# Head of a causal-convolution MLP: the first convolutions in 64x64 TensorE tiles, and B split like A

## The chip, the cores and the metric

One core of a Trainium2 chip (trn2) runs the whole program as one launch. The metric is device time in microseconds (us); the median of three runs before the change is 2223.6 us. Engines: PE is TensorE (matmul), PEld its weight loads, DVE VectorE, ACT ScalarE, POOL GpSimd, SP the queue that issues the transfers.

## The reference

```python
# x [8, 4096, 192], weight [8, 7]; w_in [192, 2048], w_out [2048, 192]; s, b scalars
w = softmax(weight, axis=-1)               # seven taps for each of 8 heads of 24 channels
x_unf = x_pad[:, idx, :]                   # causal: six zeros ahead of each sequence
out = np.einsum('hk,bskhg->bshg', w, x_unf).reshape(B * S, D)
h = out @ w_in
r = np.maximum(h, 0.0)
g = s * (r * r) + b
return (g @ w_out).astype(np.float32)
```

A depthwise causal convolution with seven taps along the sequence, then a two-layer MLP with a squared ReLU, all in float32.

## The kernel before

Channels lie on partitions, tokens along the free axis. The 32768 tokens are taken 1024 at a time (`Tokens(n)`, 32 of them), each as two blocks j = 0, 1 of 512. The 192 channels are A (channels 0 to 127) and B (the last 64). For B both blocks share a tile, `xB`: block 0 on partitions 0 to 63, block 1 on 64 to 127.

A product in float32 is made of three products in the fast type (fp32r): an operand is split into a high part (a cast) and a low part (operand less high part). The weights come as float64 bits, in eight pairs p of 256 hidden units, and `Widen` splits each on the chip in five steps: `magnitudes` (ACT), `top` (three DVE instructions), `his` (ACT casts), `low` (two on DVE), `los` (lows, DVE); `rest` is low and los. For pair 0 this is done in two parts, columns 0 to 383 for w_in (`w0`) and the rest for w_out (`w0out`).

`first(n, j, p)` is one product with w_in: 18 matmuls of 64 rows, two at a time in the two halves of the array, in the order A straight (`sA`), B, A swapped (`wA`). The swapped tile holds the other half of the channels on each half of the partitions; SP makes it with two transfers (`swap`). The result `h` has two buffers in PSUM, and ACT's `relu` frees one. Then `square` (ACT) and a cast make the high part, `lows` (DVE) the low part, and `second(n, j, p)` multiplies with w_out, with a lag of two results (`LAG`). `second_B` does the B columns of w_out later for n >= 2, in 64x64 tiles.

For n = 0 the weights become ready while they are used: `head()` writes out the first pairs' work by hand, and `pair(p)` the later ones: two firsts, the next pair's `rest`, ReLU, square and cast of both, `magnitudes` and `top` of the pair after, two seconds. `convolve(k)` puts k steps of the next tokens' convolution between: seven DVE instructions for A, seven for B (`accA`, `accB`), then the split. DVE, ACT, PE and, in the head, SP issue strictly in the order in which the code is written (`in_order`).

In the head before, PE convolves B and block 1 of A with diagonal 128x128 float32 weights (seven matmuls of 512 columns each, ACT makes the diagonals), DVE convolves block 0 of A, and PE makes low parts with a matmul by minus identity (`minus`). B's split for these tokens and the next (`split_B_at_once`) copies the halves of the partitions with ACT and DVE, so that `tB` and `wB` of block 0 need no transfer.

Of the kernel before, what the change touches and what calls it, by code (L numbers as in the profile page):

```python
# [9 lines left out]
F32 = mybir.dt.float32  # L10
# [7 lines left out]
P = 128  # L18
# [9 lines left out]
WARM = (BLK, BLK // 2, BLK // 2)  # L28
# [3 lines left out]
GAP = 40  # L32
# [13 lines left out]
def conv_attention_then_squared_relu_mlp(  # L46
# [96 lines left out]
    class Tokens:  # L143
# [7 lines left out]
        def load(self):  # L151
            n = self.n
            t0 = n * SUP
            self.xA = xin.tile([P, PAD + SUP], F32, name="xA")
            self.xB = xin.tile([P, PAD + BLK], F32, name="xB")
            skip = PAD if t0 % seq == 0 else 0
            if skip:
                nc.gpsimd.memset(self.xA[:, 0:PAD], 0.0)
# [28 lines left out]
        def split_A(self, j, acc):  # L187

            s = self.sA[j] = xs.tile([P, 2, BLK], F32R, name="sA", bufs=3)
            self.wA[j] = xs.tile([P, 2, BLK], F32R, name="wA", bufs=3)  # L190
            nc.scalar.copy(s[:, 0, :], acc)
            yield
            nc.vector.tensor_tensor(
                s[:, 1, :], acc, s[:, 0, :].bitcast(F32), op=ALU.subtract
            )
# [3 lines left out]
        def split_B(self, acc):

            self.tB = xs.tile([P, 2, BLK], F32R, name="tB")
            self.wB = xs.tile([P, 2, BLK], F32R, name="wB")
            hiB = xs.tile([P, BLK], F32R, name="hiB", bufs=1)
            nc.vector.tensor_copy(hiB, acc)
            yield
            for j in range(2):
                r = slice(j * DB, (j + 1) * DB)
                nc.vector.tensor_copy(self.tB[0:DB, j, :], acc[r, :])
                nc.vector.tensor_tensor(
                    self.tB[DB:P, j, :], acc[r, :], hiB[r, :].bitcast(F32), op=ALU.subtract  # L210
                )
                if j == 1:
                    self.swap(self.wB, self.tB)
                    self.begun = True
                yield

        def split_B_at_once(self, acc):

            self.tB = xs.tile([P, 2, BLK], F32R, name="tB")
            self.wB = xs.tile([P, 2, BLK], F32R, name="wB")  # L220
            hiB = xs.tile([P, BLK], F32R, name="hiB", bufs=1)
            nc.scalar.copy(hiB, acc)
            for j in range(2):
                r = slice(j * DB, (j + 1) * DB)
                places = (self.tB, self.wB) if j == 0 else (self.tB,)
                for k, to in enumerate(places):
                    nc.scalar.copy(to[k * DB :][0:DB, j, :], hiB[r, :].bitcast(F32))
                for k, to in enumerate(places):
                    nc.vector.tensor_tensor(
                        to[(1 - k) * DB :][0:DB, j, :], acc[r, :], hiB[r, :].bitcast(F32),  # L230
                        op=ALU.subtract,
                    )
                if j == 1:
                    self.swap(self.wB[:, 1, :], self.tB[:, 1, :])
                self.begun = True
                yield

        def split_tensor(self, acc, hi, meanwhile=None):

            nc.scalar.copy(hi, acc)  # L240
            if meanwhile:
                meanwhile()
            nc.tensor.matmul(acc, minus, hi, start=False, stop=True, skip_group_check=True)
            return lambda to, rows: nc.scalar.copy(to, acc[rows, :])
# [22 lines left out]
        def conv_tensor(self, acc, diag, x, taps=range(K)):  # L267

            for k in taps:
                nc.tensor.matmul(  # L270
                    acc, diag[:, k, :], x[:, k : k + BLK], start=k == 0, stop=k == K - 1
                )
# [96 lines left out]
    def room_for(dtype):  # L369
# [33 lines left out]
    def head():  # L403
# [9 lines left out]
        w0, w0out, w1 = Widen(0, 0, CI), Widen(0, CI, CT), wide[1]  # L413

        def diagonal(w):
            d = room_for(F32).rearrange("p a (k f) -> p (a k) f", f=P)
            for k in range(K):
                nc.scalar.activation(d[:, k, :], ident, AF.Identity, scale=w[:, k : k + 1])
# [18 lines left out]
        wB = one.wB = xs.tile([P, 2, BLK], F32R, name="wB")
        hiB = xs.tile([P, BLK], F32R, name="hiB", bufs=1)
        lo = one.split_tensor(accB, hiB, lambda: one.conv_tensor(acc1, diagA, one.xA[:, BLK:], range(0, 2)))
        one.conv_tensor(acc1, diagA, one.xA[:, BLK:], range(2, K))  # L440
        next(split)
        fetch(2)
# [11 lines left out]
        w1.los()
        nc.scalar.copy(tB[top, 1, :], hiB[bottom].bitcast(F32))

        def second_block():
            sA = one.sA[1] = xs.tile([P, 2, BLK], F32R, name="sA", bufs=3)
            wA = one.wA[1] = xs.tile([P, 2, BLK], F32R, name="wA", bufs=3)
            lo1 = one.split_tensor(acc1, sA[:, 0, :])  # L460
            one.swap(wA[:, 0, :], sA[:, 0, :])
            lo(tB[bottom, 1, :], bottom)
            one.swap(wB[:, 1, :], tB[:, 1, :])
            lo1(sA[:, 1, :], slice(0, P))
            one.swap(wA[:, 1, :], sA[:, 1, :])
# [29 lines left out]
    wide = {p: Widen(p, 0, CT) for p in range(1, NPAIR)}  # L495
# [82 lines left out]

    def square(at, cast):
        q, g = at  # L580
        nc.scalar.activation(q, q, AF.Square)  # L581
# [376 lines left out]
```

## Time and profile before

| | |
|---|---|
| runs | 2223.6, 2223.56, 2223.77 us; median 2223.6 |
| the profiled execution | 2224.18 us, its span 2222.4 us |
| granted TensorE clock | 1.00 |
| PE busy | 2216.2 us, 100% of the span |
| DVE busy | 1740.7 us, 78% |
| ACT busy | 1317.7 us, 59% |
| POOL busy | 303.9 us, 14% |

Times in the views are from the span's start. A busy PE is matmuls with modelled ends, so that the distance between two starts says more than the busy time. Shares over the whole span say little of the first 100 us, where the weights are made.

### The profile page before, as it was taken

The page shows a single profiled execution, that of the slowest core. Times are in us where ns is not written, and L with a number is a line of the kernel's source. Part 1 is how long each engine was busy: PE and PEld are TensorE (multiplying, and loading weights), DVE is VectorE, ACT ScalarE, POOL GpSimd, SP SyncE. Part 2 cuts the span into 40 slices and gives each one's busy share as a digit, 9 for nine tenths or more (in the row PEclk, how much of TensorE's full clock was granted, in tenths as well). Part 3 has the DMA queues.
Part 4 walks back from the last instruction along what each step waited for, and adds up shares of the span by engine and source line. Part 5 has one row for each costly group of instructions (what it writes and reads, how often), then busy time and mean ns, then how long its engine had stood idle before and what let it go on. Part 6 is the DMA issues. An engine that isn't in the chain of part 4 may idle for free.

```text
span 2222.4 us, 44638 instructions
## 1 busy us (share of the span) xinstructions
PE 2216.2 (100%) x19334; PEld 1610.3 (72%) x19334; DVE 1740.7 (78%) x1988; ACT 1317.7 (59%) x1424; POOL 303.9 (14%) x199
## 2 busy tenths in 40 slices
PE   9999999999999999999999999999999999999999
PEld 6788777777777777777877777777777777777776
DVE  8898777787777878778787777887787877878754
ACT  8759555565555665555655556555566555665554
POOL 0001111011111011111111101111111111011110
PEclk9999999999999999999999999999999999999999
DMA  5113212112121121211111111112112121121110
GB/s 181 30 36 93 56 51 58 51 47 55 47 58 48 44 58 44 58 51 51 48 53 49 53 50 47 53 49 63 46 46 57 45 58 49 46 56 39 44 30 17
DMA packets 46165, 117.49 MB, mean 53 GB/s; under 512 B 7760, under 2 KB 8016, under 8 KB 45968
## 3 DMA queue, kind: packets, MB, share of 16 engines
q1 hardware_dynamic: 45824, 114.50, 18.6%
q8 instruction: 151, 2.47, 0.5%
q14 instruction: 46, 0.38, 0.1%
q10 hardware_dynamic: 144, 0.13, 0.0%
HBM read 31.64 MB, written 25.17 MB: 26 GB/s over the span
## 4 chain that ended last, share of the span: by engine, by line
PE 97%; DVE 2%; ACT 1%; DMA 0%; issue 0%; SPq 0%; DVEq 0%
PE h L550 46%; PE acc L718 29%; PE acc L737 18%; PE acc L662 2%; PE h L737 0%; DVE accA L176 0%; DVE ql L587 0%; ACT q L581 0%; PE acc L632 0%; PE acc L638 0%; PE acc L640 0%; PE acc L639 0%; ACT q L573 0%; DMA xA<-in_xA 0%; DVE q L328 0%; DVE q L342 0%
## 5 line engine op out<-in xcount | busy, mean ns | idle before, releaser
L573 ACT ACTIVATE q<-h 128x1024 f32<-128x1024 f32 x512 | 526.0, 1027 | 562.9 <-PE h L550 561.0
L587 DVE TENSOR_TENSOR ql<-q,qh 128x1024 fp32r<-128x1024 f32 x498 | 666.6, 1339 | 56.2 <-ACT qh L583 4.8
L583 DVE CAST qh<-q 128x1024 fp32r<-128x1024 f32 x482 | 344.2, 714 | 360.9 <-ACT q L581 357.5
L718 PE MATMUL acc<-qh,W 64*128 64x512 f32 x3816 | 588.4, 386 | 0.0
L581 ACT ACTIVATE q<-q 128x1024 f32<-128x1024 f32 x512 | 543.5, 1062 | 16.1
L550 PE MATMUL h<-sA,W 64*128 64x512 f32 x3072 | 436.4, 389 | 0.0
L550 PE MATMUL h<-wA,W 64*128 64x512 f32 x3072 | 432.1, 386 | 0.0
L550 PE MATMUL h<-wB,W 64*128 64x512 f32 x1536 | 430.5, 387 | 0.0
L550 PE MATMUL h<-tB,W 64*128 64x512 f32 x1536 | 430.4, 387 | 0.0
L718 PEld LDWEIGHTS acc<-qh,W 64*128 64x128 f32 x3816 | 357.9, 184 | 75.6 <-issue 0.8
L737 PE MATMUL acc<-q,WB 64*64 64x512 f32 x3776 | 412.1, 591 | 0.0
L718 PE MATMUL acc<-ql,W 64*128 64x512 f32 x1908 | 371.7, 386 | 0.0
L550 PEld LDWEIGHTS h<-sA,W 64*128 64x128 f32 x3072 | 285.6, 184 | 83.9 <-issue 24.7
L550 PEld LDWEIGHTS h<-wA,W 64*128 64x128 f32 x3072 | 288.4, 184 | 60.2
L737 PEld LDWEIGHTS acc<-q,WB 64*64 64x64 f32 x3776 | 141.5, 133 | 254.7 <-issue 254.7
L176 DVE SCALAR_TENSOR_TENSOR accA<-xA,tap,accA 128x512 f32<-128x512 f32 x378 | 313.0, 828 | 5.7
L550 PEld LDWEIGHTS h<-tB,W 64*128 64x128 f32 x1536 | 282.8, 184 | 40.7 <-issue 0.2
L550 PEld LDWEIGHTS h<-wB,W 64*128 64x128 f32 x1536 | 282.9, 184 | 20.3
L727 POOL TENSOR_TENSOR outs<-outs 128x512 f32<-128x512 f32 x59 | 94.9, 1609 | 1223.4 <-ACT outs L726 1223.4
L718 PEld LDWEIGHTS acc<-ql,W 64*128 64x128 f32 x1908 | 179.0, 184 | 37.5
L176 DVE SCALAR_TENSOR_TENSOR accB<-xB,tap,accB 128x512 f32<-128x512 f32 x186 | 167.4, 900 | 6.3
L749 POOL TENSOR_TENSOR outs<-outs 128x512 f32<-128x512 f32 x59 | 107.2, 1817 | 199.1 <-ACT outs L748 198.8
(147 smaller groups left out, 891.4 us busy)
## 6 DMA issues: line engine op xcount, KB each, us to landing
wA<-sA SPq DMA_DIRECT2D x126, 256.0 KB, 3.6
outT<-outs SPq DMA_DIRECT2D x62, 256.0 KB, 2.0
wB<-tB SPq DMA_DIRECT2D x60, 256.0 KB, 3.4
xA<-in_xA SPq DMA_DIRECT2D x24, 515.0 KB, 3.6
outT<-outs SPq DMA_DIRECT2D x65, 128.0 KB, 2.2
xB<-in_xB SPq DMA_DIRECT2D x32, 259.0 KB, 3.0
outs<-outs SPq DMA_DIRECT2D x60, 128.0 KB, 2.7
outs<-in_w SPq DMA_DIRECT2D x7, 768.0 KB, 6.1
```

Source lines behind the costliest of these rows:

```text
L176: nc.vector.scalar_tensor_tensor(acc, src, w[:, k : k + 1], acc, op0=ALU.mult, op1=ALU.add)
L550: nc.tensor.matmul(h[:, i, :], w_in(w, p, chunk[0], rows), chunk[part], start=start, stop=stop)
L573: nc.scalar.activation(q, h, AF.Relu)
L581: nc.scalar.activation(q, q, AF.Square)
L583: cast(qh, q)
L587: nc.vector.tensor_tensor(ql, q, qh.bitcast(F32), op=ALU.subtract)
L662: nc.tensor.matmul(accs[to + 2 * i][0:cols], w(f, r), q[r, f % 2, :], start=start and f == 0, stop=stop and f == NF - 1,)
L718: nc.tensor.matmul(accs[i], w(f, r), q[r, f % 2, :], start=f == 0 and lo == 0, stop=f == ends[i] and lo == 2,)
L727: nc.gpsimd.tensor_tensor(o, o, o2, op=ALU.add)
L737: nc.tensor.matmul(accs[r.start // HB][i * DB : (i + 1) * DB], WB[r, p, i, :], q[r, i, :], start=p == 0, stop=p == NPAIR - 1, skip_group_c ...
L749: nc.gpsimd.tensor_tensor(o, o, o2, op=ALU.add)
```

## The change

The first convolutions, of A and B, all go to PE in 64x64 tiles. A diagonal needs only its two 64x64 blocks, so `diagonal` is now one DVE multiplication of 448 elements a partition. Straight tiles (rows to the same half of the output) serve A, crossed tiles (rows to the other half) serve B, one tap of both being four matmuls in the four quarters of the array. Block 1 of A is cut into two halves of 256 tokens; the second is fetched with swapped halves (`xS`), so that it too goes through crossed tiles. The weights of pair 0 are fetched ahead of the tokens, those of pair 1 ahead of A's second block, those of pair 2 before the head. The warm-up matmuls are 512 and six times 256 columns instead of 512 and two.

B is split in place like A for all tokens (`sB`, swapped by SP to `wB`): one ACT cast, one DVE subtraction, two transfers of 64 x 1024 words. Pair 2's weights are widened in two parts, in another order. `minus`, `hiB`, `tB` go; `GAP` keeps the size of the pool ahead of the others.

```diff
-WARM = (BLK, BLK // 2, BLK // 2)
+WARM = (BLK,) + 6 * (BLK // 2,)
+HALF = BLK // 2
-GAP = 40
+GAP = 160
 # Tokens.load, n == 0
+            if n == 0:
+                fetch(0, 0, CI)
             nc.sync.dma_start(self.xB, xB[n])
...
             if n == 0:
-                fetch(0, 0, CI)
-                nc.sync.dma_start(self.xA[:, cut:], xA[:, BLK:SUP])
+                fetch(1)
+                self.xS = room_for(F32).rearrange("p a b -> p (a b)")[:, 0 : PAD + HALF]
+                nc.sync.dma_start(self.xA[:, cut : cut + HALF], xA[:, BLK : BLK + HALF])
+                for i in range(2):
+                    to, of = (slice(k * HB, (k + 1) * HB) for k in (i, 1 - i))
+                    nc.sync.dma_start(self.xS[to], xA[of, BLK + HALF - PAD : SUP])
+        def lo(self, s, acc, cols=slice(0, BLK)):
+            nc.vector.tensor_tensor(
+                s[:, 1, cols], acc, s[:, 0, cols].bitcast(F32), op=ALU.subtract)
+        def split(self, kind, j, acc):
+            s, w = self.parts(kind, j)
             nc.scalar.copy(s[:, 0, :], acc)
             yield
+            self.lo(s, acc)
+            self.swap(w, s)
             yield
 # steps(): B of every later token
-                    yield from (self.split_B_at_once if self.n == 1 else self.split_B)(acc)
+                    yield from self.split("B", 0, acc)
+                    self.begun = True
+        def tap_tensor(self, acc, diag, x, k, swapped):
+            n = acc.shape[1]
+            for i in range(2):
+                r, o = (slice(h * HB, (h + 1) * HB) for h in (i, 1 - i if swapped else i))
                 nc.tensor.matmul(
+                    acc[o], diag[r, k, :], x[r, k : k + n],
+                    start=k == 0, stop=k == K - 1, skip_group_check=True,
                 )
 # head()
-        one.conv_tensor(accB, diagB, one.xB)
-        for _ in one.conv(acc0, one.xA, tapA, BLK):
-            pass
+        for k in range(K):
+            one.tap_tensor(acc0, diagA, one.xA, k, False)
+            one.tap_tensor(accB, diagB, one.xB, k, True)
+        for k in range(K):
+            one.tap_tensor(acc1[0], diagA, one.xA[:, BLK:], k, False)
+            one.tap_tensor(acc1[1], diagS, one.xS, k, True)
...
+        nc.scalar.copy(wB[:, 0, :], accB)
+        nc.scalar.copy(sA[:, 0, :], acc0)
+        one.lo(wB, accB)
+        one.lo(sA, acc0)
+        nc.sync.dma_start(sB[0:HB].bitcast(F32), wB[HB:P].bitcast(F32))
+        one.swap(wA, sA)
+        nc.sync.dma_start(sB[HB:P].bitcast(F32), wB[0:HB].bitcast(F32))
+        w1.los()
+        w2.magnitudes()
...
-        ha = first(0, 0, 0, second_block)
+        ha = first(0, 0, 0)
+        w0out.low()
+        q = relu(ha)
+        square_of(q)
         w0out.his()
-        q = relu(ha)
-        w0out.rest()
-        wide[2].magnitudes()
-        wide[2].top()
+        ha = first(0, 0, 1)
+        a1 = relu(ha)
         fetch(3)
         start_tokens(1)
         fetch(4)
-        ha = first(0, 0, 1)
-        a1 = relu(ha)
-        put(0, 0, 0, square(q, nc.vector.tensor_copy))
+        q = cast_of(q, nc.vector.tensor_copy)
+        put(0, 0, 0, q)
+        w0out.los()
         hb = first(0, 1, 0)
-        wide[2].low()
+        w2.top()
+        w2.his()
         b0 = squares(hb, nc.scalar.copy)
         put(0, 1, 0, b0)
-        wide[2].his()
-        wide[2].los()
+        w2.rest()
+        w2out.magnitudes()
+        w2out.top()
+        w2out.his()
         hb = first(0, 1, 1)
         put(0, 0, 1, square(a1, nc.scalar.copy))
+        w2out.rest()
```

The order on ACT behind the first ReLU of the head, before. L573 is `relu`, L581 `square`, L583 the cast of a squared result, L317 `magnitudes`, L335 `his`:

```order
L573 ACTIVATE q<-h 128x1024
L317 ACTIVATE q<-outs 128x768
L573 ACTIVATE q<-h 128x1024
L581 ACTIVATE q<-q 128x1024
L573 ACTIVATE q<-h 128x1024
L581 ACTIVATE q<-q 128x1024
L583 CAST qh<-q 128x1024
L335 CAST W<-q 128x640
```

And now, from the same ReLU on (L551 `relu`, L558 `square`, L567 cast, L292 `magnitudes`, L310 `his`):

```order
L551 ACTIVATE q<-h 128x1024
L558 ACTIVATE q<-q 128x1024
L310 CAST W<-q 128x256
L310 CAST q<-q 128x2x64
L551 ACTIVATE q<-h 128x1024
L310 CAST W<-q 128x384
L551 ACTIVATE q<-h 128x1024
L558 ACTIVATE q<-q 128x1024
L567 CAST qh<-q 128x1024
L292 ACTIVATE q<-outs 128x384
L310 CAST W<-q 128x256
L310 CAST q<-q 128x2x64
```

The square of the first result moved ahead of the second ReLU, and casts of pair 2's weights (the fourth and the last two L310) now stand ahead of the third ReLU and of the fourth, where before they stood behind a cast of a result.

The same place on DVE before: L583 casts the first squared result, L587 makes low parts, L328 ends pair 2's `top`, L341 and L342 are its `low`, L348 its `los`:

```order
L325 TENSOR_SCALAR q<-q 128x768
L328 SCALAR_TENSOR_TENSOR q<-outs,q 128x768
L583 CAST qh<-q 128x1024
L587 TENSOR_TENSOR ql<-q,qh 128x1024
L341 TENSOR_SCALAR q<-q 128x768
L342 SCALAR_TENSOR_TENSOR q<-outs,q 128x768
L587 TENSOR_TENSOR ql<-q,qh 128x1024
L348 TENSOR_TENSOR W<-q,W 128x640
```

And now (L567 cast, L571 lows, L323 and L325 `los`, L296 to L303 `top`, L316 `low`):

```order
L567 CAST qh<-q 128x1024
L571 TENSOR_TENSOR ql<-q,qh 128x1024
L323 TENSOR_TENSOR W<-q,W 128x256
L323 TENSOR_TENSOR q<-q 128x2x64
L325 TENSOR_TENSOR W<-W,q 128x256
L325 TENSOR_TENSOR q<-q 128x2x64
L296 TENSOR_SCALAR q<-q 128x384
L300 TENSOR_SCALAR q<-q 128x384
L303 SCALAR_TENSOR_TENSOR q<-outs,q 128x384
L571 TENSOR_TENSOR ql<-q,qh 128x1024
L316 TENSOR_SCALAR q<-q 128x384
```

Pair 2's `top` stood ahead of the cast of the first result and now stands behind it and behind the lows of pair 0's w_out.

The third place is SP at the split of B for tokens 1, before:

```order
L184 DMA wA<-sA 64x1024
L185 DMA wA<-sA 64x1024
L160 DMA xB<-in_xB 128x518
L185 DMA wB<-tB 64x512
L184 DMA wB<-tB 64x512
L163 DMA xA<-in_xA 128x1030
```

And now:

```order
L191 DMA wA<-sA 64x1024
L192 DMA wA<-sA 64x1024
L163 DMA xB<-in_xB 128x518
L191 DMA wB<-sB 64x1024
L192 DMA wB<-sB 64x1024
L166 DMA xA<-in_xA 128x1030
```

The places are the same; the two transfers of B now carry both blocks, where before block 0 had needed none.

More of the change, by code (lines that the diff above doesn't have):

```diff
@@ L185, in swap, with parts @@
             nc.sync.dma_start(to[HB:P], of[0:HB])
-        def split_A(self, j, acc):
-            s = self.sA[j] = xs.tile([P, 2, BLK], F32R, name="sA", bufs=3)
-            self.wA[j] = xs.tile([P, 2, BLK], F32R, name="wA", bufs=3)
+        def parts(self, kind, j=0):
+            s, w = (xs.tile([P, 2, BLK], F32R, name=x + kind, bufs=3 - (kind == "B")) for x in "sw")
+            if kind == "A":
+                self.sA[j], self.wA[j] = s, w
+            else:
+                self.sB, self.wB = s, w
+            return s, w
@@ L197, in split_A @@
             yield
[L199 to L244, printed above, removed]
         def half(self, j, i):
             r = slice(i * HB, (i + 1) * HB)
-            b = (self.tB, self.wB) if i == 0 else (self.wB, self.tB)
+            b = self.sB if i == j else self.wB
@@ L260, in steps @@
                 yield from self.conv(acc, self.xA[:, j * BLK :], tapA, BLK)
-                yield from self.split_A(j, acc)
+                yield from self.split("A", j, acc)
                 if j == 0:
@@ L413, in head, with diagonal @@
         w0, w0out, w1 = Widen(0, 0, CI), Widen(0, CI, CT), wide[1]
[L415 to L418, printed above, removed]
-            return d
-        top, bottom = slice(0, DB), slice(DB, P)
-        diagB = diagonal(tapB)
+        w2, w2out = Widen(2, 0, CI), Widen(2, CI, CT)
+        def diagonal(place, k):
+            d = place.rearrange("p (k f) -> p k f", f=DB)[:, 0:K]
+            shape = [P, K, DB]
+            nc.vector.tensor_tensor(
+                d, fold.unsqueeze(1).to_broadcast(shape),
+                tap[:, k, :].unsqueeze(2).to_broadcast(shape), op=ALU.mult,
+            )
+            return d
@@ L423, in head @@
+        two = room_for(F32)
+        diagA, diagB = diagonal(two[:, 0, :], 0), diagonal(two[:, 1, :], 1)
+        diagS = diagonal(room_for(F32)[:, 0, :], 2)
         accB = ps_o.tile([P, BLK], F32, name="acc2")
-        acc1 = ps_o.tile([P, BLK], F32, name="acc1")
-        one.conv_tensor(accB, diagB, one.xB)
-        acc0 = xs.tile([P, BLK], F32, name="accA")
-        for _ in one.conv(acc0, one.xA, tapA, BLK):
-            pass
-        nc.scalar.mul(minus, ident, -1.0)
-        diagA = diagonal(tapA)
+        acc0 = ps_o.tile([P, BLK], F32, name="acc1")
@@ L431, in head @@
+        acc1 = [ps_o.tile([P, BLK], F32, name=f"acc{k}")[:, 0:HALF] for k in (2, 1)]
+        for k in range(K):
[4 more added lines that the diff above has]
+            one.tap_tensor(acc1[1], diagS, one.xS, k, True)
         w0.magnitudes()
-        split = one.split_A(0, acc0)
-        next(split)
         w0.top()
         w0.his()
-        tB = one.tB = xs.tile([P, 2, BLK], F32R, name="tB")
@@ L437, in head @@
[L437 to L442, printed above, removed]
+        w0.rest()
         w1.magnitudes()
-        w0.rest()
         w1.top()
-        nc.scalar.copy(tB[top, 0, :], hiB[top].bitcast(F32))
-        nc.scalar.copy(wB[bottom, 0, :], hiB[top].bitcast(F32))
@@ L448, in head @@
-        lo(tB[bottom, 0, :], top)
-        lo(wB[top, 0, :], top)
-        w1.his()
         w1.low()
         w0out.magnitudes()
-        w0out.top()
[L454 to L465, printed above, removed]
@@ L468, in head @@
-        ha = first(0, 0, 0, second_block)
+        w1.his()
+        sB, wB = one.parts("B")
+        sA, wA = one.parts("A", 0)
+        nc.scalar.copy(wB[:, 0, :], accB)
[7 more added lines that the diff above has]
+        w2.magnitudes()
+        s1, w1A = one.parts("A", 1)
@@ L469, in head @@
+        for k, c in enumerate((slice(0, HALF), slice(HALF, BLK))):
+            nc.scalar.copy(s1[:, 0, c], acc1[k])
+        for k, c in enumerate((slice(0, HALF), slice(HALF, BLK))):
+            one.lo(s1, acc1[k], c)
+        one.swap(w1A, s1)
+        w0out.top()
+        ha = first(0, 0, 0)
+        w0out.low()
+        q = relu(ha)
+        square_of(q)
         w0out.his()
-        q = relu(ha)
-        w0out.rest()
-        wide[2].magnitudes()
-        wide[2].top()
+        ha = first(0, 0, 1)
@@ L493, in head @@
         convolve(CONV[1])
-    wide = {p: Widen(p, 0, CT) for p in range(1, NPAIR)}
+    wide = {p: Widen(p, 0, CT) for p in range(1, NPAIR) if p != 2}
     def column_sums(k):
@@ L942 @@
         "xB": xB,
[L943 removed]
+        "taps": np.ascontiguousarray(
+            np.stack([taps[:P], np.tile(taps[P:], (2, 1)), np.roll(taps[:P], P // 2, 0)], axis=1)
+        ),
         "w": np.concatenate([w_in, *w_out], axis=2),
```

35 lines of the change are left out of this document (17 added, 18 removed).

## The prediction

> **What bounds the kernel now.** I read the page's busy times first, then the chain of work that ended last, then the first 100 us engine by engine in order of time. The page's PE line, a row of the table by stage (columns: stretch, its length, busy time of PE, PEld, DVE, ACT, POOL, clock, DMA share, GB/s) and rows of the chain:
>
> ```profile
> PE 2216.2 (100%) x19334; PEld 1610.3 (72%) x19334; DVE 1740.7 (78%) x1988; ACT 1317.7 (59%) x1424; POOL 303.9 (14%) x199
> 32.70:60.00 27.30, 27.30 (x188) 20.68 (x188) 25.73 (x38) 25.70 (x30) 0.00 (x0) 1.00 0.25 84
> 30.50 0.68 PE acc L632 x2
> 288.68 13.89 PE acc L737 x128
> 302.57 2.30 PE h L550 x18
> ...
> 313.04 2.04 PE h L550 x18
> ```
>
> From about 100 us on nothing but PE counts: the chain is unbroken matmuls, a first takes 2.04 us for nine pairs, and the 0.26 us more after each second_B (2.30) is the one seam. The new kernel has the same matmuls there, so a delay or gain of the head goes to the end one to one. But from 32.7 to 60 us DVE and ACT are 94% busy beside PE, and the chain comes to PE only at 30.5 us, from DVE's lows. In the head three engines are nearly full, and order among them decides. PE's rows that I use as marks (start, length; L550 is a first, 34.89 that of pair 2's second block, 55.19 pair 5's, 91.95 the B part of the first one of tokens 1):
>
> ```profile
> 0.99 3.54 PE L410 MATMUL acc<-q 128*128 128x512 f32 x6 [0.99 <-POOL xA L158]
> 4.49 6.25 PE L270 MATMUL acc<-xB,q 128*128 128x512 f32 x14
> 34.89 0.85 PE L550 MATMUL h<-sA,W 64*128 64x512 f32 x6
> 55.19 0.84 PE L550 MATMUL h<-sA,W 64*128 64x512 f32 x6
> 91.95 0.62 PE L550 MATMUL h<-wB,W 64*128 64x512 f32 x2
> ```
>
> Six matmuls are three pairs at 0.23 us, so 0.69 us of array and 0.16 us until the last can be read. Transfers (landing of the first tokens; data rate in slices of a quarter microsecond over 0 to 10 us; two swaps with time to landing, and their issues):
>
> ```profile
> 1.65 3.79 DMA xA<-in_xA
> GB/s 0 0 0 0 0 0 0 28 34 83 58 149 166 315 379 362 389 352 438 430 332 266 274 311 328 193 205 254 336 418 406 406 442 406 467 418 394 222 124 99
> wA<-sA SPq DMA_DIRECT2D x1, 256.0 KB, 3.4
> wA<-sA SPq DMA_DIRECT2D x1, 256.0 KB, 3.7
> 12.67 0.54 SPq L184 DMA_DIRECT2D wA<-sA  x1
> 13.26 0.59 SPq L185 DMA_DIRECT2D wA<-sA  x1
> ```
>
> The second swap lands 0.59 + 3.7 - 3.4 = 0.9 us behind the first: queued swaps take 0.9 us each. ACT (casts, ReLU L573, square L581, magnitudes L317):
>
> ```profile
> 12.07 0.51 ACT L335 CAST W<-q 128x384 fp32r<-128x384 f32 x1 [0.64 <-DVE q L328]
> 20.43 0.41 ACT L335 CAST W<-q 128x256 fp32r<-128x256 f32 x1
> 20.74 0.30 ACT L335 CAST q<-q 128x128 fp32r<-128x128 f32 x1
> 21.37 1.03 ACT L573 ACTIVATE q<-h 128x1024 f32<-128x1024 f32 x1 [0.33 <-PE h L550]
> 26.62 1.06 ACT L581 ACTIVATE q<-q 128x1024 f32<-128x1024 f32 x1
> 27.71 1.05 ACT L583 CAST qh<-q 128x1024 fp32r<-128x1024 f32 x1
> 28.67 0.72 ACT L335 CAST W<-q 128x640 fp32r<-128x640 f32 x1
> 31.55 0.91 ACT L317 ACTIVATE q<-outs 128x768 f32<-128x768 f32 x1
> 32.36 1.01 ACT L573 ACTIVATE q<-h 128x1024 f32<-128x1024 f32 x1
> 33.40 1.06 ACT L581 ACTIVATE q<-q 128x1024 f32<-128x1024 f32 x1
> 88.97 0.62 ACT L222 CAST hiB<-accB 128x512 fp32r<-128x512 f32 x1 [1.95 <-DVE accB L176]
> ```
>
> Starts are 0.09 us ahead of the end before where the next does not need it. DVE (low part of A; low and los of 384 columns from 12.56 to 14.48; top of 768 and low to 18.13; top of 384 to 19.48; los of w_out from 22.26 to 23.41; cast and lows of a result):
>
> ```profile
> 11.96 0.68 DVE L193 TENSOR_TENSOR sA<-accA,sA 128x512 fp32r<-128x512 f32 x1
> 12.56 0.35 DVE L341 TENSOR_SCALAR q<-q 128x384 int32<-128x384 int32 x1
> 14.48 0.55 DVE L321 TENSOR_SCALAR q<-q 128x768 f32<-128x768 f32 x1
> 18.13 0.36 DVE L321 TENSOR_SCALAR q<-q 128x384 f32<-128x384 f32 x1
> 19.40 0.82 DVE L348 TENSOR_TENSOR W<-q,W 128x640 fp32r<-128x640 f32 x1
> 22.26 0.42 DVE L348 TENSOR_TENSOR W<-q,W 128x256 fp32r<-128x256 f32 x1
> 23.13 0.28 DVE L350 TENSOR_TENSOR q<-q 128x128 fp32r<-128x128 f32 x1
> 25.91 0.69 DVE L583 CAST qh<-q 128x1024 fp32r<-128x1024 f32 x1
> 26.63 1.23 DVE L587 TENSOR_TENSOR ql<-q,qh 128x1024 fp32r<-128x1024 f32 x1
> 32.24 1.22 DVE L587 TENSOR_TENSOR ql<-q,qh 128x1024 fp32r<-128x1024 f32 x1
> 54.50 0.82 DVE L350 TENSOR_TENSOR W<-W,q 128x640 fp32r<-128x640 f32 x1
> ```
>
> **Part 1, up to the first ReLU (R): earlier.** xA lands at 5.44 before; 384 KB of weights now stand ahead of it on SP, 1.05 us at some 375 GB/s, so 6.5. The warm-up's 1024 columns take 3.5 us; the conv's fourteen records (two a matmul) show half that price a column (6.25 us for 7 x 512), so four more of 256 end near 6.3, and PE waits little. The three diagonals have no row; the nearest, L348 with 640 columns, is 0.82 us, so I take 0.62 each for 448; they start at 3.9 and are under the wait for xA. At twice that, pair 0's top waits behind them and R comes 1.2 later; a gain is excluded by that wait.
>
> The 64x64 float32 matmul is priced by second_B: 128 records, 64 matmuls, 13.89 us, 0.217 us each with four in the array; alone it is the conv's 0.89. I take 0.217, since four quarters are used here too. So 28 x 0.217 = 6.1, to 12.6, and the half-width 28 in 3.0, to 15.7 (at no saving from the half width 18.7, R + 0.8). Low end nothing, high end is a rival below. Off PE fall 14 large matmuls and two by minus identity, off DVE 5.2 us of convolution, off ACT 14 diagonals and ten small copies: gone, but not on this path any more.
>
> Weights of pair 1 (768 KB) land at 8.5, magnitudes 0.9, top and low on DVE 14.48 to 18.13 = 3.65, so both engines are free at 13.1. Then cast of accB 0.62 (to 13.4), its low 0.68 (14.1), A's low 0.6 (14.7). SP sends B's first half at 14.1, landing 17.5, and A's two at 14.7 and 15.3, landing 18.4 and 19.3. PE does A's straight part to 16.4, waits 1.1 for B, and 1.1 for wA, ends at 20.0: **R = 20.2**, before 21.37, 1.2 us sooner. With swaps 1 us faster it is 19.2. Queued behind these swaps are only B's other half and block 1's (wanted at 22.7 and 23.4, landing by 20.2 and 22), then pair 3's weights, wanted at 37. POOL does nothing new.
>
> **Part 2, R to pair 2: much later.** Here DVE and ACT take turns. In the new order DVE's cast of the first result waits for its square; behind that cast stand its lows, los of w0out, and top of pair 2; ACT's casts of pair 2 wait for that top, and behind them stand the other block's ReLU, square and cast, for which DVE's next lows wait, and so on once more:
> - ReLU 1.04 (32.36 to 33.40) and square 1.09 (26.62 to 27.71): R + 2.15. DVE cast 0.72, lows 1.14, los 1.06, top 1.35 (18.13 to 19.48): R + 6.4.
> - ACT cast of 384 columns 0.5, ReLU 1.04, square 1.09, cast 1.05: R + 10.1. PE's second of that block starts then, at 30.3, and its low part is there at 31.5; the four firsts and one second are over at 28.6. That wait is hidden by the next.
> - DVE lows 1.14, rest of 384 columns 1.92 (12.56 to 14.48), top of w_out 1.35: R + 14.5. ACT casts 0.5, square 1.09, cast 0.96 to the next start, magnitudes 0.81, ReLU 1.01: R + 18.9.
>
> That last ReLU frees the buffer of pair 2's second first. It can start at R + 19.0 = 39.2 and started at 34.89: **4.3 us late** in spite of the sooner R, with PE idle for some 3.1 us before it.
>
> **Part 3, to pair 5.** From the lows of a1 on DVE has no gap. They start when their cast ends, R + 14.5 + 0.5 + 1.09 + 1.05 = 37.4; before, 32.24. To these 5.2 come 1.9 for the rest of w_out of pair 2, done apart now (los 1.06 and low 0.86), so DVE is 7.0 late with a small gap of before filled. Pair 5's low weights were ready at 54.50 + 0.82 = 55.32 and wanted at 55.19 + 0.46 = 55.65: slack 0.3. PE comes **6.7 us late** to pair 5. Nothing gives it back, as PE was dense from there.
>
> **Part 4, B of tokens 1.** accB is cast at 88.97; now 6.7 later, 95.7. Cast 0.62, low 0.68, to 97.0 with hand-overs. The second transfer of the swap is issued 0.55 later and lands after 3.7: 101.2. PE asks for it at 91.95 + 6.7 = 98.65 and **waits 2.6 us**, where tB and wB had needed no transfer. Bounds: nothing, if the swap were early by that much, and 3.0. Three ACT copies and two DVE subtractions fewer are off this path. For later tokens four DVE instructions fewer and one ACT cast more lie under PE's dense rows (2.04 us each), and the swap of B goes out a step sooner: nothing.
>
> **Sum.** 6.7 + 2.6 = 9.3 us, of which part 2 is 4.3, part 3 2.4. The profiled execution took 2224.18 (span 2222.4 and 1.8 around it), 0.6 over the median; with 9.3 it is 2233.5, and as a median 2232.9; I say 2233. With R, swaps and seams at their favourable ends it is 7.5, at the others 12: 2231 to 2235.6.
>
> **Rivals.** (a) Serial tiles. Both straight tiles write one bank from different halves of the rows, while second_B gives each half of the rows a bank of its own, so its row does not show this case. If two of the four wait for each other, part 1 takes 12.2 and 6.1 instead of 6.1 and 3.0: PE starts its first at 24.8, no swap is late, R = 24.8 + 2.06 + 0.16 = 27.0, 6.8 later, and all else follows: 2239.8. For it: no row with such a pair. Against: the two write different partitions. [...]
>
> (b) The clock. The opening matmuls cost twice a column for 3.5 us. If PE's wait of 3.1 us before pair 2's second block brings that state back, another 3.5 us at half speed cost 1.75: 2234.7. Before has no such wait. [...]
>
> (c) The early start is kept, and the kernel is faster. DVE is idle from pair 0's last low, about 19.5, to R + 2.15 = 22.3; if pair 2's top (1.35) were done there, ACT's casts would not wait and the firsts, ending 1 us sooner, would carry it through: 2222.6. It decides if top ends before the second ReLU does, R + 3.7 = 23.9. Against it: top stands behind the cast in the written order, and the rows of before start in that order everywhere.
>
> (d) The turns cost less: PE late by under 7.4 us in all because part 4's swap is met or DVE has slack that I don't see: 2228.1 to 2231.
>
> **How the numbers follow.** Forecast 0.70, (a) 0.12, (b) 0.06, (c) 0.04, (d) 0.08. The range leaves out (a) and (c): 2229 to 2237.5; the likeliest case's own is 2231 to 2235.6. A change under 0.2%, 4.4 us, can't be told from none. Slower holds all but (c) and a little of (d): 0.95; same 0.02, faster 0.03.
>
> **What would show it.** Right: R near 20.2; ACT's cast of 384 columns released by DVE L303 near R + 6.5; PE idle some 3 us until near 39 for the ReLU of ACT L551; pair 5's first some 6.7 us late, waiting for DVE L325; a PE wait of 2 to 3 us for the B swap near 100; equal rows after. Wrong: conv records of 64x64 spaced over 0.12 us (a), ACT's casts of pair 2 not waiting (c), or B's swap there before PE.

## The result, and the profile after

The changed kernel takes 2236.80 us (median of six runs, 2236.45 to 2237.85), the kernel before on the same chip 2223.62: a ratio of 1.006, 95% interval [1.0047, 1.0073], 13.2 us slower. The profiled execution took 2236.45 (span 2234.4), so 12.3 more than the profiled one of before and 12.0 in the span; the sums below are made against those 12.0. Two of the later kernels, the eighth and the ninth, have a profiled execution that ran at a granted clock of 0.95 and 0.75 from end to end, so it is left out of their medians.

First the page's busy times, and a table by stage, cut where the granted clock changes and 3.42 us ahead of each stretch at half clock (columns as in the prediction; the clock, as a share of full speed, stands behind POOL):

```profile
PE 2218.7 (99%) x19424; PEld 1631.9 (73%) x19424; DVE 1667.9 (75%) x1873; ACT 1324.2 (59%) x1432; POOL 304.3 (14%) x199
4.68:38.81 34.13, 28.08 (x231) 17.40 (x229) 22.74 (x45) 16.20 (x25) 0.00 (x0) 1.00 0.66 212
38.81:42.23 3.42, 1.50 (x14) 1.24 (x16) 3.20 (x8) 3.36 (x5) 0.00 (x0) 1.00 0.03 5
42.23:45.64 3.41, 3.41 (x13) 2.08 (x10) 3.34 (x5) 2.01 (x4) 0.00 (x0) 0.50 0.62 225
100.25:103.67 3.42, 1.02 (x9) 0.55 (x8) 0.74 (x1) 0.68 (x1) 0.00 (x0) 1.00 0.50 129
103.67:107.08 3.41, 3.41 (x20) 2.66 (x18) 0.00 (x0) 1.57 (x2) 0.00 (x0) 0.50 0.02 5
```

DVE does 72.8 us less than before (1740.7 to 1667.9), and the kernel is slower: what was saved lay beside PE. After each of two stretches in which PE is busy for less than half (1.50 and 1.02 us of 3.42) comes one of 3.41 us at half clock. PE's waits in the head, and its marks (the longest waits in total, then starts of firsts, now L528; 62.63 is pair 5's, 99.43 that of tokens 1):

```profile
PE h L528 <- ACT q L551: 3.0, 1, 3.0
PE h L528 <- DMA wB<-sB: 2.4, 1, 2.4
...
40.73 0.96 PE L528 MATMUL h<-sA,W 64*128 64x512 f32 x6 [3.00 <-ACT q L551]
62.63 0.70 PE L528 MATMUL h<-sA,W 64*128 64x512 f32 x4
63.97 0.51 PE L528 MATMUL h<-sA,W 64*128 64x512 f32 x2 [0.64 <-DVE W L325]
99.43 0.97 PE L528 MATMUL h<-sA,W 64*128 64x512 f32 x6
103.03 0.50 PE L528 MATMUL h<-wB,W 64*128 64x512 f32 x1 [2.40 <-DMA wB<-sB]
```

Pair 2's second block starts 5.8 us later than before (34.89), pair 5's first 7.4 (55.19), its last two straight matmuls, behind a wait for DVE, 8.3 (63.97 against some 55.65), the first one of tokens 1 8.3 (91.15 before). Then come the 2.4 of the wait, and 1.3 for the half clock behind it: seven firsts on (129.57 against 117.70), the kernel is 11.9 late, and so it stays to the end.

The turns of ACT and DVE, as the trace shows them (ACT, then DVE; the brackets give the idle time ahead and what ended it):

```profile
21.77 1.03 ACT L551 ACTIVATE q<-h 128x1024 f32<-128x1024 f32 x1 [5.36 <-PE h L528]
28.24 0.51 ACT L310 CAST W<-q 128x384 fp32r<-128x384 f32 x1 [2.94 <-DVE q L303]
36.32 0.41 ACT L310 CAST W<-q 128x256 fp32r<-128x256 f32 x1 [4.01 <-DVE q L303]
39.67 1.01 ACT L551 ACTIVATE q<-h 128x1024 f32<-128x1024 f32 x1
...
23.92 0.69 DVE L567 CAST qh<-q 128x1024 fp32r<-128x1024 f32 x1 [3.43 <-ACT q L558]
31.88 1.23 DVE L571 TENSOR_TENSOR ql<-q,qh 128x1024 fp32r<-128x1024 f32 x1 [3.67 <-ACT qh L567]
39.00 1.23 DVE L571 TENSOR_TENSOR ql<-q,qh 128x1024 fp32r<-128x1024 f32 x1 [2.71 <-ACT qh L567]
```

Whoever works, the other one is idle: DVE for 3.43, 3.67 and 2.71 us, ACT for 2.94 and 4.01.

### The profile page after: what moved, and what is told of

Read it like the earlier page. It is cut to its first block, busy times and chain, and to the rows that moved or that the text cites. A ratio compares the mean times of both kernels' runs of the same rounds, so it can differ in the third digit from the quotient of the medians.

```text
span 2234.4 us, 44704 instructions
## 1 busy us (share of the span) xinstructions
PE 2218.7 (99%) x19424; PEld 1631.9 (73%) x19424; DVE 1667.9 (75%) x1873; ACT 1324.2 (59%) x1432; POOL 304.3 (14%) x199
## 4 chain that ended last, share of the span: by engine, by line
PE 96%; DVE 2%; ACT 1%; DMA 1%; issue 0%; SPq 0%; DVEq 0%
PE h L528 46%; PE acc L702 29%; PE acc L721 18%; PE acc L646 2%; ACT q L558 0%; DVE ql L571 0%; PE h L721 0%; ACT q L551 0%; DMA outs<-in_w 0%; ACT qh L567 0%; DMA wA<-sA 0%; DVE q L303 0%; DVE q L317 0%; DMA wB<-sB 0%; ACT q L567 0%
## 5 line engine op out<-in xcount | busy, mean ns | idle before, releaser
L551 ACT ACTIVATE q<-h 128x1024 f32<-128x1024 f32 x512 | 526.2, 1028 | 557.3 <-PE h L528 555.8
L571 DVE TENSOR_TENSOR ql<-q,qh 128x1024 fp32r<-128x1024 f32 x498 | 666.5, 1338 | 63.8 <-ACT qh L567 12.3
L567 DVE CAST qh<-q 128x1024 fp32r<-128x1024 f32 x482 | 364.9, 757 | 443.7 <-ACT q L558 442.1
L558 ACT ACTIVATE q<-q 128x1024 f32<-128x1024 f32 x512 | 543.5, 1061 | 16.0
L528 PE MATMUL h<-sA,W 64*128 64x512 f32 x3072 | 443.4, 390 | 3.6 <-ACT q L551 3.0
L528 PE MATMUL h<-wA,W 64*128 64x512 f32 x3072 | 440.1, 387 | 1.1 <-DMA wA<-sA 1.1
L528 PE MATMUL h<-wB,W 64*128 64x512 f32 x1536 | 430.9, 387 | 2.4 <-DMA wB<-sB 2.4
L528 PE MATMUL h<-sB,W 64*128 64x512 f32 x1536 | 431.1, 387 | 1.6 <-DMA sB<-wB 1.6
L702 PEld LDWEIGHTS acc<-qh,W 64*128 64x128 f32 x3816 | 362.8, 184 | 74.0 <-issue 0.8
L528 PEld LDWEIGHTS h<-sA,W 64*128 64x128 f32 x3072 | 293.6, 184 | 84.7 <-issue 24.3
L528 PEld LDWEIGHTS h<-wA,W 64*128 64x128 f32 x3072 | 296.9, 184 | 59.0 <-DMA wA<-sA 1.9
L183 DVE SCALAR_TENSOR_TENSOR accA<-xA,tap,accA 128x512 f32<-128x512 f32 x372 | 308.3, 829 | 5.5
L528 PEld LDWEIGHTS h<-sB,W 64*128 64x128 f32 x1536 | 282.9, 184 | 31.4 <-DMA sB<-wB 2.0
L528 PEld LDWEIGHTS h<-wB,W 64*128 64x128 f32 x1536 | 282.8, 184 | 31.1 <-DMA wB<-sB 2.8
```

Of the source, the lines that this page charges most:

```text
L183: nc.vector.scalar_tensor_tensor(acc, src, w[:, k : k + 1], acc, op0=ALU.mult, op1=ALU.add)
L528: nc.tensor.matmul(h[:, i, :], w_in(w, p, chunk[0], rows), chunk[part], start=start, stop=stop)
L551: nc.scalar.activation(q, h, AF.Relu)
L558: nc.scalar.activation(at[0], at[0], AF.Square)
L567: cast(qh, q)
L571: nc.vector.tensor_tensor(ql, q, qh.bitcast(F32), op=ALU.subtract)
```

## The experiments

All are edits of the changed kernel, five rounds each, beside runs of the kernel before on the same chip (its medians were 2223.59, 2223.81 and 2223.61).

**1. The first turn out.**

```diff
         w0out.low()
+        w2.top()
         q = relu(ha)
...
         hb = first(0, 1, 0)
-        w2.top()
         w2.his()
```

> The changed kernel with pair 2's top for w_in (three DVE instructions, 1.35 us) moved ahead of the first result's cast, into the 3.43 us in which DVE waits for the first square. Theory A (the loss of the head is the turns of DVE and ACT, an order): the first turn goes, pair 2's second first falls from 40.73 to about 37.9, pair 5's from 62.62 to about 59.8, and the time by 2.8 us, to 2234.0; the second turn and the wait for B's swap stay, with the half clock behind the latter. Theory B (DVE simply has more to do up to pair 5, whatever the order): pair 5's first stays within 0.7 us of 62.62 and the time within 0.7 us of 2236.8.

Measured: 2235.23 us (2233.75 to 2235.83), ratio 1.0051 [1.0038, 1.0063]; 1.6 less than the changed kernel, between the two theories. The profiled execution is the slowest of the five. Its table, and PE's and ACT's rows:

```profile
15.16:18.57 3.41, 1.80 (x24) 0.92 (x16) 3.41 (x9) 0.98 (x3) 0.00 (x0) 1.00 0.63 133
18.57:25.40 6.83, 6.39 (x29) 4.22 (x29) 3.77 (x9) 2.57 (x4) 0.00 (x0) 0.50 1.00 268
...
40.21 0.96 PE L528 MATMUL h<-sA,W 64*128 64x512 f32 x6 [2.98 <-ACT q L551]
...
22.63 1.02 ACT L551 ACTIVATE q<-h 128x1024 f32<-128x1024 f32 x1 [6.11 <-PE h L528]
26.05 1.03 ACT L551 ACTIVATE q<-h 128x1024 f32<-128x1024 f32 x1 [0.81 <-PE h L528]
28.12 1.03 ACT L551 ACTIVATE q<-h 128x1024 f32<-128x1024 f32 x1 [0.64 <-PE h L528]
```

ACT's wait for pair 2's top is gone. But here PE's own firsts ran at half clock from 18.57 to 25.40, and ACT waits 0.81 + 0.64 us for them. Pair 2's second first comes 40.21 - 22.63 = 17.6 us behind the first ReLU, against 18.96 in the changed kernel: 1.4 sooner, where 2.8 were expected and 1.45 went to the slow firsts. The two quickest runs (2233.75, 2234.01) stand at the 2234.0 of theory A, but pair 5's first starts at 62.03, within theory B's 0.7 us of 62.62. By itself this run leaves theory B open; the next one does not.

**2. Both turns out.** Besides the first edit:

```diff
         w2.his()
-        b0 = squares(hb, nc.scalar.copy)
-        put(0, 1, 0, b0)
         w2.rest()
+        b0 = relu(hb)
+        square_of(b0)
         w2out.magnitudes()
+        put(0, 1, 0, cast_of(b0, nc.scalar.copy))
         w2out.top()
-        w2out.his()
         hb = first(0, 1, 1)
         put(0, 0, 1, square(a1, nc.scalar.copy))
+        w2out.his()
         w2out.rest()
```

> As the first, and the second turn taken out too: pair 2's low and lows for w_in stand ahead of the second result's lows on DVE, the magnitudes of its w_out columns ahead of that result's cast on ACT, and the casts of those columns behind the next square. Theory A: no PE wait of over 0.5 us from the firsts to pair 5 but those for a first's own result; pair 2's second first near 35.5, pair 5's near 55.5 to 56, the time 7.2 us less than the changed kernel's, 2229.6; the granted clock is 1.00 from 5 to 90 us, since the wait of 3 us is gone, and half speed only behind the wait for B's swap. Theory B: pair 5's first above 60 and the time above 2234. If the half clock is not due to the wait ahead of it, the first stretch of it is still there between 35 and 50.

Measured: 2229.77 us (2228.36 to 2232.68, nine runs), ratio 1.0027 [1.0018, 1.0037]: 7.0 less, where A said 7.2. Nothing was taken away here; the same instructions stand in another order. Theory B is out. PE's longest wait, and the table around the first ReLU and around the wait for B's swap:

```profile
PE h L529 <- DMA wB<-sB: 2.4, 1, 2.4
...
17.79:21.21 3.42, 1.85 (x11) 1.02 (x13) 3.23 (x9) 0.00 (x0) 0.00 (x0) 1.00 1.00 237
21.21:24.62 3.41, 3.41 (x20) 2.68 (x18) 0.84 (x2) 2.40 (x4) 0.00 (x0) 0.50 0.99 258
...
92.89:96.30 3.41, 2.16 (x12) 1.20 (x10) 2.18 (x4) 2.22 (x4) 0.00 (x0) 1.00 0.85 218
96.30:99.72 3.42, 2.28 (x20) 1.96 (x22) 0.00 (x0) 0.59 (x1) 0.00 (x0) 1.00 0.06 14
```

The wait for ACT's ReLU is gone, that for B's swap is as long as it was, and yet the clock stays at 1.00 behind it: it lies from 95.05 to 97.44, across two of the stretches shown, and PE is busy for 2.16 of the 3.41 us of the first (63%) and for 2.28 of the 3.42 of the second (67%). From the first wB matmul to the fourth first of these tokens it is 105.42 - 97.44 = 7.98 us, in the changed kernel 112.27 - 103.03 = 9.24: the half clock there costs **1.26 us**.

One thing expected did not come: the clock is not 1.00 from 5 to 90 us. In place of the stretch at half clock behind pair 2's wait, which is gone, there is one from 21.21, behind the waits for the first swaps. Two firsts start 25.02 - 21.54 = 3.48 us apart there instead of 2.05; pair 2's second first comes at 36.73 and pair 5's at 57.02, each 1 us or more later than expected, and pair 5's 1.1 us later than in experiment 4's trace (55.92), which has no such stretch. These 1.1 us and the 1.26 not lost behind B's wait about cancel, so that 7.0 is still a fair price of the order.

**3. No swap for the half of B that is wanted first.**

```diff
             nc.scalar.copy(s[:, 0, :], acc)
+            if kind == "B" and self.n == 1:
+                nc.scalar.copy(w[HB:P, 0, :], s[0:HB, 0, :].bitcast(F32))
             yield
             self.lo(s, acc)
-            self.swap(w, s)
+            if kind == "B" and self.n == 1:
+                nc.vector.tensor_tensor(
+                    w[HB:P, 1, :], acc[0:HB], s[0:HB, 0, :].bitcast(F32), op=ALU.subtract
+                )
+                nc.sync.dma_start(w[0:HB].bitcast(F32), s[HB:P].bitcast(F32))
+            else:
+                self.swap(w, s)
```

> The changed kernel, but for the tokens 1024 to 2047 the swapped half of B that block 0 reads is made by one more ACT copy and one more DVE subtraction (64 rows), and only the other half by a transfer. Theory A (the wait of 2.40 us for B's swap costs itself and the half clock of 3.4 us behind it): no PE wait for wB near 103, granted clock 1.00 from 99 to 110, the time 2.4 + 1.5 less, 2232.9. Theory C (the clock goes back for another reason than the wait, the load of the stage itself): the wait goes, the half clock stays, 2234.4. If the transfer is hidden anyway in the sum (another wait takes its place), no more than 1 us less.

Measured: 2233.24 us (2232.65 to 2233.76), ratio 1.0043 [1.0031, 1.0056]: 3.6 less. The table from tokens 1 on, and PE's rows there:

```profile
99.70:110.00 10.30, 10.30 (x91) 8.19 (x92) 7.62 (x12) 8.16 (x9) 0.00 (x0) 1.00 0.13 29
...
99.70 0.97 PE L536 MATMUL h<-sA,W 64*128 64x512 f32 x6
100.51 0.39 PE L536 MATMUL h<-wB,W 64*128 64x512 f32 x1
```

No wait, no half clock. The next seven firsts and what stands between them take 26.5 us as before the change; in the changed kernel they take 30.1. Theory A holds, with 1.3 us for the half clock instead of 1.5: 2.4 and 1.3, together 3.7.

**4. Both.** The edits of 2 and 3.

> The second and the third together: both turns out and B's first swapped half by copies. Theory A: the parts add, 7.2 + 3.9 less than 2236.8, 2225.7; what stays over the kernel before (about 2 us) is the first ReLU of 21.77 against a schedule made for 20.2, and there is no stretch of half clock after 5 us. Theory B: above 2231. If the two gains overlap (the swap is waited for less when the head is sooner, or DVE's split comes later), 2227 to 2228.

Measured: 2225.35 us (eleven runs; nine of them 2224.94 to 2225.81, the other two 2228.57 and 2228.78 at a mean clock of 0.998), ratio 1.0011 [1.0002, 1.0020]. 11.4 of the 13.2 us are back, with the convolutions in tiles as they were. The first one of tokens 1 starts at 92.75, 1.6 us behind the 91.15 of before, and that is nearly all that is left. Of it 0.9 us are there at the first ReLU (22.30 against 21.37); the rest comes behind it, with a wait for DVE in pair 5 (L333). PE's waits, and that ReLU:

```profile
PE h L537 <- DMA sB<-wB: 1.4, 1, 1.4
PE h L537 <- DMA wA<-sA: 1.2, 2, 0.8
PE h L537 <- DVE W L333: 0.6, 1, 0.6
...
22.30 1.03 ACT L560 ACTIVATE q<-h 128x1024 f32<-128x1024 f32 x1 [5.28 <-PE h L537]
```

**5. Why the first ReLU is late: the fetch of pair 2?**

```diff
     fetch(0, CI, CT)
-    fetch(2)
...
         w1.los()
-        w2.magnitudes()
...
         one.swap(w1A, s1)
+        fetch(2)
...
         a1 = relu(ha)
+        w2.magnitudes()
```

> The changed kernel with the 768 KB of pair 2's weights fetched behind the swaps of block 1 (and their magnitudes behind the second ReLU), so that no such transfer lands while pair 1's weights are widened. Theory D (the 1.57 us by which the first ReLU came later than forecast are mostly that landing: ACT's L292 of 768 at 1.38 us instead of 0.91, DVE's L303 of 768 at 1.22 instead of 0.96): both are back at 0.91 and 0.96, the swaps go out 0.7 to 1 us sooner, the first ReLU is near 20.9 and the time 0.8 less, near 2236. Theory E (the lateness is pair 1's own landing at 9.09 and the transfers' 4.4 us to land, with or without that fetch): durations and first ReLU stay within 0.3 us of 21.77, the time within 0.5 us of 2236.8.

Measured: 2237.53 us (2236.06 to 2238.74), ratio 1.0061 [1.0048, 1.0074]: no gain. ACT's and DVE's rows, and ACT's row of experiment 1, where that fetch was in its old place:

```profile
9.86 1.32 ACT L292 ACTIVATE q<-outs 128x768 f32<-128x768 f32 x1 [2.13 <-DMA outs<-in_w]
22.52 1.02 ACT L551 ACTIVATE q<-h 128x1024 f32<-128x1024 f32 x1 [6.12 <-PE h L528]
12.40 0.98 DVE L303 SCALAR_TENSOR_TENSOR q<-outs,q 128x768 int32<-128x768 int32 x1
```
```profile
10.00 0.91 ACT L292 ACTIVATE q<-outs 128x768 f32<-128x768 f32 x1 [2.42 <-DMA outs<-in_w]
```

DVE's row is back at 0.98, but ACT's is still 1.32, pair 1's weights land no sooner, and the first ReLU is later still. Theory D falls. E's bounds are missed too, by 0.45 us at the ReLU and 0.2 in the time, but what it says of the landing fits: over the seven traces with these first swaps ACT's read of pair 1's weights starts at 9.11 to 10.00 us, and the first ReLU comes 12.5 to 12.9 us behind it in six of them (13.2 in experiment 6). No experiment moved that landing by itself. Why ACT's read takes 0.91 us in one execution and 1.38 in another stays open.

**6. The same wait with PE busy in it.**

```diff
+        if (n, j, p) == (1, 0, 0):
+            for _ in range(10):
+                both(0, 1, 0, True, True)
         for at in (0, 2, 1):
```

> The changed kernel with ten extra pairs of matmuls (2.3 us, their sums overwritten) in PE's wait for B's swap of tokens 1, ahead of that first. No transfer and no other engine's work is changed. If the half clock behind that wait comes from PE's idle share of the window before it: the wait for wB falls from 2.40 to some 0.3 to 0.8 us, all later work starts no later, the clock from 99 to 110 is 1.00, and the time is 1.3 to 1.7 less, near 2235.3. If it comes from the transfers or the stage: the half clock stays, and the time is 2236.8 or more.

Measured: 2236.36 us (2235.31 to 2237.11), ratio 1.0056 [1.0042, 1.0070]: 0.4 less, where 1.3 to 1.7 were expected. The place itself (the table, PE's rows):

```profile
102.07:105.48 3.41, 3.14 (x29) 2.23 (x27) 0.74 (x1) 0.09 (x1) 0.00 (x0) 1.00 0.34 100
105.48:108.90 3.42, 3.42 (x34) 2.81 (x32) 0.65 (x1) 2.77 (x3) 0.00 (x0) 1.00 0.00 0
...
100.65 3.26 PE L528 MATMUL h<-sA,W 64*128 64x512 f32 x26
104.41 0.49 PE L528 MATMUL h<-wB,W 64*128 64x512 f32 x1 [0.27 <-DMA wB<-sB]
```

The pairs did what was said: the wait is 0.27, the clock 1.00, and from the wB matmul to the fourth first 112.39 - 104.41 = 7.98 us again. In this execution the total missed because 1.2 us were lost by 100.65 (99.43 in the changed kernel): its first ReLU is at 23.01 (21.77 there), with a mean granted clock of 0.89 over the first 30 us where the changed kernel has 1.00. The quickest of the five runs has the 2235.3 that was expected; the others have no trace. In the changed kernel the 2.40 us lay from 100.63 to 103.03, with the half clock from 103.67. Only that idle time was taken away here, and the clock stayed at 1.00. That the wait, left in, would have brought the half clock in this execution too is the author's estimate: the same wait of 2.4 us goes with a mean clock of 0.91 from 90 to 110 us in the changed kernel and in experiments 1 and 5, but with 1.00 in experiment 2.

**7. The first swaps sooner, and DVE's wait filled.** On top of 4: `wB`'s and `sA`'s casts and `lo` ahead of pair 1's `his` and `low`, and

```diff
         w2.top()
+        w2.low()
         q = relu(ha)
...
         w2.his()
-        w2.rest()
+        w2.los()
```

> The fourth experiment's kernel (both turns out, B's half by copies), and the casts and low parts of the two convolutions moved ahead of pair 1's casts and low parts on ACT and DVE, and pair 2's low for w_in (0.92 us) moved into DVE's wait for the first square. Theory A (the 1.8 us that stay over the kernel before are the late first ReLU and a dense DVE behind it): the swaps go out near 14 instead of 15.1, the first ReLU is 0.8 to 1.1 us sooner than 22.3 to 21.8, pair 5's first near 54.9 to 55.2, and the time 2224.0 to 2224.4. [...]

Measured: 2224.59 us (2224.05 to 2226.92, eleven runs), ratio 1.0005 [0.9996, 1.0014]: 0.8 under experiment 4, no longer to be told from before. The issue of the first swap, the first ReLU, and PE's row in pair 5:

```profile
13.98 0.50 SPq L435 DMA_DIRECT2D sB<-wB  x1
20.61 1.03 ACT L561 ACTIVATE q<-h 128x1024 f32<-128x1024 f32 x1 [4.33 <-PE h L538]
55.64 0.50 PE L538 MATMUL h<-sA,W 64*128 64x512 f32 x2 [0.64 <-DVE W L333]
```

The swaps go out 1.2 us sooner, and the ReLU comes 1.2 sooner than in the changed kernel, 1.7 sooner than in experiment 4's trace. The first one of tokens 1 starts at 91.09, where it was at 92.75 and, before, at 91.15: in the profiled executions the gain is 1.7 us, in the medians 0.8. PE still waits 0.64 us for DVE in pair 5.

**8. Pair 2's weights whole again.** On top of 7: pair 2 in the buffer that pair 1 leaves, `magnitudes`, `top`, `his` and `low` once for all 768 columns, the second result's lows ahead of `los`.

> The seventh experiment's kernel with pair 2's weights widened whole again up to the low part (768 columns at once, in the buffer that pair 1 leaves, so that the top fits into DVE's wait for the first square), the lows of the second result ahead of its los. DVE issues about 1 us less between the first cast and pair 5 (two tops of 1.27 to 1.35 and two lows of 0.92 become one of 1.9 and one of 1.4). If DVE is what still holds pair 5's second block (PE wait of 0.6 us there for its lows), pair 5 comes 0.6 to 1 us sooner than 57.35, without that wait, and the time is 2223.6 to 2224.0, the kernel before's. If ACT's chain from the first ReLU sets it instead, 2224.6 as the seventh.

Measured: 2223.57 us (median of eleven, 2223.24 to 2225.94): 1.0 less than experiment 7, and level with the 2223.61 of before. That DVE's extra instructions for the split in two parts held pair 5 fits this time, but three things were changed at once (the split, the buffer, the place of the lows), and no trace at full clock shows which of them counted.

**9. The first swaps in high and low parts.** On top of 8:

```diff
+        def sent(k):
+            nc.sync.dma_start(sB[0:HB, k, :].bitcast(F32), wB[HB:P, k, :].bitcast(F32))
+            one.swap(wA[:, k, :], sA[:, k, :])
+        sent(0)
         one.lo(wB, accB)
         one.lo(sA, acc0)
-        nc.sync.dma_start(sB[0:HB].bitcast(F32), wB[HB:P].bitcast(F32))
-        one.swap(wA, sA)
+        sent(1)
```

> As the eighth, and the three swaps that the first first waits for are cut into high and low parts, the high ones sent as soon as they are cast: six transfers of 128 KB instead of three of 256 KB. If a transfer's landing goes with its size (2.3 us for 128 KB against 3.7 for 256 KB later in the trace), the last lands 0.7 to 1 us sooner, the first ReLU is near 19.8 instead of 20.6, and the time 0.1 to 0.7 under the eighth's, 2223.0 to 2223.8; below 2223.2 it would beat the kernel before. If SP's issues (0.6 us each) and the queue eat it, the same as the eighth.

Measured: 2223.06 us (median of eleven, 2222.38 to 2223.94), before 2223.61, ratio 0.9999 [0.9990, 1.0008]. The median is 0.5 us under before's and 13.7 under the changed kernel's, but the interval takes in no difference; that it beats the kernel before is not shown. The profiled execution does show the gain: from the start of accB's cast to the first ReLU, which comes behind the swaps, it is 22.07 - 15.14 = 6.9 us against 20.91 - 12.95 = 8.0 in the eighth's.

## Why the prediction was right

The forecast was 2233, slower; measured 2236.8. Sign, places and the main mechanism were right; the sum of 9.3 us was 12.0. The time lies inside the stated range of 2229 to 2237.5, but 0.8 us from its end and outside the 2231 to 2235.6 given for the likeliest case: two misses went the same way, one of them a cost that the sum did not have. That they stayed inside is in part luck.

- **Part 1, the price of the tiles:** right. The first half's 28 matmuls (two records each, a row of A and a row of B for each tap's half) start between 6.46 and 12.53, 6.07 us: 0.217 us each, 0.108 a record:

```profile
6.46 0.65 PE L244 MATMUL acc<-xA,q 64*64 64x512 f32 x2
6.47 0.65 PE L244 MATMUL acc<-xB,q 64*64 64x512 f32 x2
...
12.53 0.38 PE L244 MATMUL acc<-xA,q 64*64 64x256 f32 x2
```

  Start 6.46 (forecast 6.5), end of the first half 12.5 (12.6), start of the first behind it 15.66 (15.7). Rival (a) is out: two tiles of different row halves that write one bank do not wait for each other here, since with two of the four waiting the first half was to take 12.2 us, and its starts lie within 6.07.
- **Part 1, the first ReLU:** the step that failed in size, 21.77 instead of 20.2, so that nothing came sooner at all. The rows:

```profile
outs<-in_w SPq DMA_DIRECT2D x1, 768.0 KB, 6.5
...
9.11 1.38 ACT L292 ACTIVATE q<-outs 128x768 f32<-128x768 f32 x1 [1.32 <-DMA outs<-in_w]
11.71 1.22 DVE L303 SCALAR_TENSOR_TENSOR q<-outs,q 128x768 int32<-128x768 int32 x1
15.14 0.50 SPq L429 DMA_DIRECT2D sB<-wB  x1
...
wA<-sA SPq DMA_DIRECT2D x1, 256.0 KB, 4.4
```

  Pair 1's weights landed at 9.1, not 8.5; ACT's magnitudes took 1.38, not 0.9; DVE's top and low took 3.9, not 3.65. The swaps were issued 1.0 us later than forecast, and the three took 3.0, 3.7 and 4.4 to land, so that they came 1.3 us apart where the sum had 0.9. The prediction had no row for these landings: the first it put by rate alone, the others it carried on from one pair of swaps (3.4 and 3.7). Its sum also slips: 13.1 and 0.62 make 13.7, not 13.4. The slip didn't tell, since the cast of accB (13.79 to 14.37) was over before DVE was free (14.44).
- **Part 2, the turns:** right to a tenth. From the first ReLU on, top's end was forecast at 6.4, the second block's cast at 10.1, the next top at 14.5, the ReLU that frees the buffer at 18.9 and PE at 19.0; the trace has 6.44, 10.07, 14.52, 18.91 and 18.96.
- **Part 3:** right with the ReLU's lateness put in. The lows of a1 start at 39.00, 6.76 behind before (forecast 5.2, and 1.57 of the ReLU). At the first one of tokens 1 it is 8.28 (forecast 6.7, and 1.57). Experiment 2 shows that the order made it.
- **Part 4:** 2.40 us instead of 2.6; experiment 3 takes it away.
- **Rival (b), the clock:** given 0.06; the half clock came, twice, but its price did not come where it was looked for. Behind pair 2's wait it seems to have cost nothing that counts, since PE still waits 0.64 us for DVE in pair 5. Behind B's wait, where the prediction put nothing, it cost 1.26 us. Half clock came behind a wait of 2.40 us in the changed kernel, and in experiment 2 it did not come behind one of 2.4.
- **Rival (c)** did not come by itself, but its edit is experiment 1: the top does fit into DVE's idle time, yet alone it brings 2235.2 and not the 2222.6 that (c) put on it. **(d)** did not come.

So 6.7 + 2.6 became 8.3 + 2.4 + 1.3 = 12.0: 1.6 are the first ReLU, 1.3 the clock, -0.2 the swap.

## What to carry to other kernels

When two engines that are each nearly full feed one another in a fixed order, trace the hand-overs one by one: three us of idle time on either side at each turn is a loss that another order can take away, as 7.0 of 13.2 us here. Work moved off an engine gains nothing where it lay beside the bound (72.8 us of DVE's here), but a transfer put in the place of a copy must be covered by work already queued: B's swaps took some 3.7 us to land in the changed kernel (median of 62), and PE waited 2.40 us for the first. And a PE wait can cost more than itself: the 2.40 us brought 1.26 more in the changed kernel's trace, a wait of 2.4 us in experiment 2's nothing.

## What the runs showed of the hardware that was not expected

The length of a wait did not decide alone whether half clock followed. From 4.68 to 120 us of the changed kernel's trace the granted clock fell to 0.50 twice, for 3.41 us each time, and in the 3.42 us ahead PE had been busy for 1.50 us (44%) and 1.02 us (30%). Three more such falls: 6.83 us in experiment 1, behind 1.80 of 3.41 us (53%), 3.41 us in experiment 2, behind 1.85 of 3.42 (54%), and 3.41 us in experiment 3, behind 1.25 of 3.41 (37%):

```profile
29.86:33.27 3.41, 1.25 (x5) 0.46 (x3) 1.16 (x2) 2.62 (x4) 0.00 (x0) 1.00 0.52 208
33.27:36.68 3.41, 3.29 (x8) 2.54 (x9) 3.11 (x8) 0.13 (x1) 0.00 (x0) 0.50 0.02 5
```

But the clock stayed at 1.00 behind 1.59 of 3.41 us (47%, 35.64 to 39.05) in experiment 1, and in the changed kernel behind 1.85 of 3.41 (54%, 14.92 to 18.33) and 1.91 of 3.42 (56%, 28.57 to 31.99). Nor do like waits end alike: PE waited 2.98 us for ACT's ReLU in experiment 1, with a clock of 1.00 from 30 to 90 us, and 3.00 us in the changed kernel, with half clock from 42.23; and the wait of 2.4 us for B's swap goes with a mean clock of 0.91 from 90 to 110 us in the changed kernel and in experiments 1 and 5, with 1.00 in experiment 2. What decides was not shown.

The times of the runs, beside their mean clocks, spread by 0.7 us in 23 runs of the kernel before, where PE's longest wait from 5 to 130 us is 0.7 us and the mean clock is 1.00 in every run, and by 1.4 in six of the changed one, at 0.997 to 0.999; in experiment 4 two runs, at 0.998, lie 3.3 and 3.5 us above the median of the other nine, at 1.00.
